# A first block of 512 tokens that starts with its first 256, and diagonals built by ScalarE in six pairs

## The chip, the cores and the metric

The kernel runs on one core of one Trainium2 chip. The metric is the device time of one execution in microseconds (us). Three runs of the kernel before gave 998.15, 998.85 and 999.84 us; the median is 998.85 us.

## The reference

Three parts run one after the other: a linear attention with a decaying state, and two small dense networks.

```
# r, k, v, w: batch 4, heads 8, 768 tokens, head width 48;  u: heads x 48
for t in range(S):
    cur   = outer(u * k[t], v[t])
    y[t]  = r[t] @ (state + cur)
    state = w[t][:, None] * state + outer(k[t], v[t])
x = y as 3072 tokens x 384
x = ((x @ w_a) * (x @ w_b)) @ w_out        # 384 -> 1536 -> 384
h = max(x @ w_in, 0);  x = (h * h) @ w_out2 # 384 -> 2048 -> 384
```

## The kernel before, in words

**Attention.** The 3072 tokens are 24 pairs of two chunks of 64 tokens. For a pair, VectorE (DVE in the rows) forms running products of the decay w (`at_scan`, L248) and their inverses (`at_recip`, L253, four instructions); GpSimd (POOL) multiplies them into k (`at_kr`, L257) and r (`at_rr`, L261). TensorE (PE) forms the scores (tile `sc`, L288 and L289), the transposed keys (`kt`, L299), the state's growth (`ds`, L311 and L313) and the outputs (`yp`, L332 and L333). The term with u needs one number per token and head: GpSimd multiplies r, k and u (L270), VectorE sums over the head (`dg`, L274), and GpSimd spreads the sums onto diagonals of the tile `ar` (`at_diag`, L278); VectorE then copies the scores above the diagonal into `ar` (`at_A2`, L294). `at_C2` (L320 to L324) carries the state to the next chunk.

**Weights.** The weights come as 64-bit floating-point words and are taken apart on the chip. The first network has 12 units (one per feature tile of 128), each with the words of w_a, w_b and w_out for that tile. A unit takes seven instructions of 128x1152: three by ScalarE (ACT; `z`, `raw`, then `w`, all L176) and four that change the bits (L191, L195, L200) or subtract (L209): L191 and L195 by VectorE, L200 and L209 by VectorE or GpSimd. L209 (`dec_lo`) is the last; TensorE can use the unit's tile `w` after it.

**Networks.** Every factor is split into a high and a low part, so one product takes three matmuls. Tokens go through in blocks: the first network's blocks are 384, 256, 384 and four times 512 tokens, the second's six times 512. For each block and feature tile, TensorE runs 9 matmuls for each of two products (tile `pa`, L358 to L360, in two PSUM buffers), ScalarE copies the first out (L365), VectorE multiplies it with the second (`mult`, L369), ScalarE and GpSimd split the result (`gh`, `gl`, L379), and 9 matmuls add it to three accumulators (`acc`, L385 to L387). The x of a block is written to DRAM by the attention, read back and split by ScalarE (`xh`) and VectorE (`xl`, L551).

**Order.** All instructions are put in order by a planner (`Plan.run`): it keeps a list of steps with engines, assumed durations, dependencies and a due time, and starts the ready step with the smallest due time whenever an engine is free. The due times come from a table of numbers (`KNOB`). What the planner starts on an engine stands in that engine's queue in this order, and each engine works its queue from front to back. A step with two engines in `ENG` goes to the one that is free first.

Of the kernel before, what the change touches and what calls it, by code (L numbers as in the profile page):

```python
# [21 lines left out]
C = 64  # L22
# [5 lines left out]
BLOCKS1 = [384, 256, 384] + [512] * 4  # L28
# [95 lines left out]
def fused_kernel(ctx, tc, tpk, natpk, vpk, v2pk, upk, cst, w1pk, w2pk, out):  # L124
# [226 lines left out]
    def prod(w, x, n):  # L351
# [4 lines left out]
        for k in range(KD):  # L356
            h, l = xh[:, k, 0:n], xl[:, k, 0:n]
# [14 lines left out]
    def split_hi(g, n, e="ACT"):  # L372
# [9 lines left out]
    def down(acc, d, w, g, n, first, last):  # L382
# [61 lines left out]
    def plan_pair(p):  # L444
# [33 lines left out]
        depA, acqA = [("kr", p), (("rr", 0), p), (("rr", 1), p)], [("at", (p, "A"))]  # L478
# [21 lines left out]
        add("B", {"PE": 0.41 * cold}, K["B"], lambda e: at_B(p), [("kr", p), "consts"], acq=[("at", (p, "B"))])  # L500
        add("B2", both(0, 448, *ENG["b2"]), K["B"], lambda e: at_B2(p, e), [("B", p)], acq=[("ky", (p, "k"))],
# [10 lines left out]
    def plan_dec(u, n, s, prio, deps):  # L512
# [7 lines left out]
        add(("ds", u, s), {"DVE": 0.75}, prio, lambda e: dec_sign(u, n), [("dz", u, s)], port=True)  # L520
# [4 lines left out]
        add(("dl", u, s), both(0, n, *ENG["dl"]), prio, lambda e: dec_lo(u, n, e), [("dh", u, s)], rel=[("z", (u, s))],  # L525
# [34 lines left out]
    def plan_step(s, j, f, nf, n, t, prev, w_up, w_down, units, dst):  # L560

        k = (s, j, f)
        need = [("dl", u, s) for u in units]
        before = (s, j, f - 1) if f else (s, j - 1, nf - 1) if j else (1, nb1 - 1, NF1 - 1) if s == 2 else ()
        add, mm, early = plan.add, 9 * t_mm(n), t - K["EARLY"]
        add(("ua", *k), {"PE": mm}, t, lambda e: put(("pa", *k), prod(part(w_up[0]), xs[s, j], n)),
            [("XS", s, j), ("ua", *before), ("ub", *before), *need], acq=[("ab", ("a", k))], rel=[] if s == 1 or f < nf - 1 else [("x", (s, j))])
        if s == 1:
# [3 lines left out]
            add(("ub", *k), {"PE": mm}, t, lambda e: put(("pb", *k), prod(part(w_up[1]), xs[s, j], n)),  # L572
                [("ua", *k)], acq=[("ab", ("b", k))], rel=[("x", (s, j))] if f == nf - 1 else [])
            add(("g", *k), both(0, n, "DVE"), early,
                lambda e: put(("g", *k), mult(box["a", *k], box["pb", *k], n)), [("a", *k), ("ub", *k), ("g", *before)],
                rel=[("ab", ("b", k))])
        else:
# [3 lines left out]
            add(("g", *k), both(0, n, "DVE"), early,  # L581
# [17 lines left out]
        if f < nf - 1:  # L599
            return  # L600
# [255 lines left out]
```

## Time and profile before

| what | us |
|---|---|
| median of three runs | 998.85 |
| profiled execution | 998.08 |
| its span | 996.2 |
| TensorE busy in the span | 940.4 (94%) |
| VectorE busy | 479.3 (48%) |
| ScalarE busy | 384.1 (39%) |
| GpSimd busy | 441.6 (44%) |

The profile covers one execution. Its span is the time from the first to the last recorded event on the core; the execution's own time is 1.9 us longer. A busy share is an average over the whole span, and the stages differ: TensorE has gaps in the first 130 us and none to speak of from there on, VectorE is the other way round. The granted clock in the windows is a share of TensorE's full speed.

### The profile page before, as it was taken

Reading aid. Unit: us, or ns where it says so; the run is one execution under the profiler, and the core shown is the slowest. Engines: PE = TensorE matmul, PEld = TensorE weight load, DVE = VectorE, ACT = ScalarE, POOL = GpSimd, SP = SyncE. Lnnn points to the kernel's source line nnn. Section 1 sums busy time; section 2 is a strip of 40 time slices with the busy share of each in tenths; the row PEclk is TensorE's granted clock in tenths of the full one; section 3 lists DMA queues with packets and bytes.
Section 4 is the critical chain, followed back from the end, with each engine's and each line's share of the span. In section 5 each row is a group of like instructions: output and inputs, shape, how many; then the busy total and the mean of one; then the engine's idle time right before and its main releaser. Section 6 shows DMA issues by size and latency. Waiting matters only on the chain.

```text
span 996.2 us, 14962 instructions
## 1 busy us (share of the span) xinstructions
PE 940.4 (94%) x5982; PEld 802.0 (81%) x5982; DVE 479.3 (48%) x585; ACT 384.1 (39%) x591; POOL 441.6 (44%) x359
## 2 busy tenths in 40 slices
PE   2668799999999999999999999999999999999997
PEld 2567699999988888888888888888888888888885
DVE  6889988875764444573212688721121211211111
ACT  1677443433422333332332677442233332323322
POOL 6733478886674545544122344333333333333332
PEclk9579899999999999999999999999999999999999
DMA  9995134652632332341111554010010000100001
GB/s 267 335 332 135 59 99 128 178 148 77 166 117 76 108 107 77 94 135 38 40 42 64 191 205 143 1 64 1 6 59 0 33 32 1 64 1 1 32 0 37
DMA packets 57791, 91.89 MB, mean 92 GB/s; under 512 B 23664, under 2 KB 31600, under 8 KB 57712
## 3 DMA queue, kind: packets, MB, share of 16 engines
q1 hardware_dynamic: 57712, 90.84, 29.6%
q8 instruction: 49, 0.80, 0.3%
q14 instruction: 30, 0.25, 0.1%
HBM read 76.66 MB, written 14.16 MB: 91 GB/s over the span
## 4 chain that ended last, share of the span: by engine, by line
PE 88%; DVE 5%; DMA 3%; ACT 1%; issue 1%; SPq 0%; POOL 0%; DVEq 0%; ACTq 0%
PE pa L358 16%; PE pa L360 16%; PE pa L359 16%; PE acc L385 11%; PE acc L387 11%; PE acc L386 11%; PE sc L288 2%; PE yp L332 2%; DVE w L209 1%; DVE z L200 1%; PE kt L299 1%; DMA ef<-in_tpk_dram 1%; PE ds L313 1%; DVE z L195 1%; DMA vs<-in_vpk_dram 1%
## 5 line engine op out<-in xcount | busy, mean ns | idle before, releaser
L379 POOL TENSOR_TENSOR gl<-a,gh 128x512 fp32r<-128x512 f32 (+2 forms) x180 | 235.2, 1308 | 474.4 <-ACT gh L176 469.9
L358 PE MATMUL pa<-xh,w 128*128 128x512 f32 (+2 forms) x792 | 296.3, 374 | 7.7 <-ACT w L176 3.3
L360 PE MATMUL pa<-xh,w 128*128 128x512 f32 (+2 forms) x792 | 295.1, 373 | 7.6 <-DVE w L209 7.6
L359 PE MATMUL pa<-xl,w 128*128 128x512 f32 (+2 forms) x792 | 294.4, 372 | 0.0
L365 ACT ACTIVATE a<-pa 128x512 f32<-128x512 f32 (+2 forms) x180 | 102.3, 569 | 277.8 <-PE pa L360 219.1
L385 PE MATMUL acc<-gh,w 128*128 128x512 f32 (+2 forms) x540 | 205.6, 381 | 0.0
L387 PE MATMUL acc<-gl,w 128*128 128x512 f32 (+2 forms) x540 | 202.7, 375 | 0.0
L386 PE MATMUL acc<-gh,w 128*128 128x512 f32 (+2 forms) x540 | 202.4, 375 | 0.0
L369 DVE TENSOR_TENSOR a<-a 128x512 f32<-128x512 f32 x96 | 67.9, 707 | 253.4 <-ACT a L365 253.4
L176 ACT ACTIVATE gh<-a 128x512 fp32r<-128x512 f32 (+2 forms) x180 | 108.3, 602 | 207.7 <-DVE a L369 161.9
L358 PEld LDWEIGHTS pa<-xh,w 128*128 128x128 f32 x792 | 150.1, 190 | 32.8 <-ACT w L176 4.3
L360 PEld LDWEIGHTS pa<-xh,w 128*128 128x128 f32 x792 | 150.2, 190 | 32.0 <-DVE w L209 9.2
L359 PEld LDWEIGHTS pa<-xl,w 128*128 128x128 f32 x792 | 150.1, 189 | 22.7 <-DVE xl L551 0.3
L369 DVE TENSOR_TENSOR a<-a,pa 128x512 f32<-128x512 f32 (+2 forms) x84 | 51.0, 607 | 140.8 <-PE pa L360 140.4
L385 PEld LDWEIGHTS acc<-gh,w 128*128 128x128 f32 x540 | 101.4, 188 | 17.9
L387 PEld LDWEIGHTS acc<-gl,w 128*128 128x128 f32 x540 | 101.5, 188 | 17.3 <-POOL gl L379 0.4
L386 PEld LDWEIGHTS acc<-gh,w 128*128 128x128 f32 x540 | 101.5, 188 | 16.2
L253 DVE RECIPROCAL ef<-ef 112x128 f32<-112x128 f32 x96 | 82.7, 913 | 0.5
L261 POOL TENSOR_TENSOR ar<-rk,ef 48x512 f32<-48x512 f32 (+1 forms) x48 | 59.0, 1230 | 27.8 <-DVE ef L248 10.0
L294 DVE COPY_PREDICATED ar<-mask,sc 64x512 f32<-64x512 int32 x48 | 35.2, 734 | 39.7 <-PE sc L289 37.7
L278 POOL TENSOR_TENSOR ar<-ident,dg 64x512 f32<-64x512 f32 x48 | 51.5, 1073 | 1.8
L209 DVE TENSOR_TENSOR w<-z,w 128x1152 fp32r<-128x1152 f32 (+1 forms) x22 | 37.2, 1691 | 6.0 <-ACT w L176 6.0
(54 smaller groups left out, 834.3 us busy)
## 6 DMA issues: line engine op xcount, KB each, us to landing
raw<-in_w1pk_dram SPq DMA_DIRECT2D x36, 384.0 KB, 6.8
raw<-in_w2pk_dram SPq DMA_DIRECT2D x32, 384.0 KB, 3.8
rk<-in_tpk_dram SPq DMA_DIRECT2D x24, 448.0 KB, 4.9
nat<-in_natpk_dram SPq DMA_DIRECT2D x24, 384.0 KB, 3.7
v<-in_v2pk_dram SPq DMA_DIRECT2D x24, 384.0 KB, 4.3
ef<-in_tpk_dram SPq DMA_DIRECT2D x24, 227.5 KB, 3.7
vs<-in_vpk_dram SPq DMA_DIRECT2D x48, 96.0 KB, 2.8
xd<-ys SPq DMA_DIRECT2D x48, 96.0 KB, 3.2
```

The lines of the kernel that those rows point to most:

```text
L176: nc.scalar.activation(out=out, in_=in_, func=ACTF.Copy, **({} if scale is None else {"scale": scale}))
L253: nc.vector.reciprocal(out=hv(inv(p), C)[:, h0:h0 + 2], in_=hv(ext(p), C + 1)[:, h0:h0 + 2, 1:])
L261: eng(e).tensor_tensor(out=hv(AR[p % 2][rows, c, :], C), in0=hv(RK[p][rows, TR:TK], C), in1=hv(ext(p), C + 1)[rows, :, 0:C], op=ALU.mult)
L358: nc.tensor.matmul(out=out, lhsT=blk(wh, k), rhs=h, start=(k == 0), stop=False)
L359: nc.tensor.matmul(out=out, lhsT=blk(wh, k), rhs=l, start=False, stop=False)
L360: nc.tensor.matmul(out=out, lhsT=blk(wl, k), rhs=h, start=False, stop=(k == KD - 1))
L365: nc.scalar.activation(out=a[:, 0:n], in_=P[:, 0:n], func=func, scale=scale)
L369: eng(e).tensor_tensor(out=a[:, 0:n], in0=a[:, 0:n], in1=b[:, 0:n], op=ALU.mult)
L379: eng(e).tensor_tensor(out=gl[:, 0:n], in0=g[:, 0:n], in1=gh[:, 0:n], op=ALU.subtract)
L385: nc.tensor.matmul(out=o, lhsT=blk(wh, d), rhs=gh[:, 0:n], start=first, stop=False)
L386: nc.tensor.matmul(out=o, lhsT=blk(wl, d), rhs=gh[:, 0:n], start=False, stop=False)
L387: nc.tensor.matmul(out=o, lhsT=blk(wh, d), rhs=gl[:, 0:n], start=False, stop=last)
```

## The change

The first network's blocks become six times 512 tokens. In the first block the first six feature tiles are done in two halves: the first 256 tokens (pairs 0 and 1) alone, the other 256 (pairs 2 and 3) later, each half with its own matmuls of 256 columns; the other six tiles are done with 512 columns. So that the accumulators start with 512 columns, the first matmul into each of the three is 512 wide, and ScalarE fills the missing half of its operand with zeros. For the first six pairs the diagonals are written by ScalarE, one 64x64 instruction for each head and chunk (16 a pair) in place of two by GpSimd, and the multiplication of k may go to VectorE. The first network's L200 and L209 (L207 and L216 in the new file) go to VectorE alone. Every due time has a new number.

```diff
-BLOCKS1 = [384, 256, 384] + [512] * 4
+BLOCKS1 = [512] * 6
+FIRST, APART = 256, 6
-KNOB = dict(START=13.52, FIRST=7.12, LEAD=18.8, DEC=4.0, DO=13.32, XO=5.1, X2=-14.73, D2=33.64, LW=15.56, LT=19.97,
+KNOB = dict(START=57.49, LEAD=22.53, DEC=8.23, U0=20.49, XO=44.77, X2=-72.12, D2=58.09, LW=19.06, LT=19.96, LV=0.24,
...
+           b2=("ACT",), gl=("POOL",), gh=("ACT",), dg=("POOL",), u1=("POOL",), ds=("DVE",))
+ENG0 = dict(ENG, kr=("DVE", "POOL"), dg=("ACT",), da=("DVE",), dl=("DVE",))
+NP0 = 6
...
     def at_diag(p, c, e="POOL"):
         rows = slice(c * C, c * C + C)
+        if e == "ACT":
+            for h in range(H):
+                nc.scalar.activation(out=AR[p % 2][rows, c, h * C:(h + 1) * C], in_=ident[rows, rows], func=ACTF.Copy,
+                                     scale=DG[p][rows, h:h + 1])
+            return
...
-            h, l = xh[:, k, 0:n], xl[:, k, 0:n]
+            h, l = xh[:, k, c0:c0 + n], xl[:, k, c0:c0 + n]
...
+        if fill:
+            copy("ACT", gh[:, n:NB], floor[:, 0:NB - n], 0.0)
...
-        o = acc[d][:, 0:n]
-        nc.tensor.matmul(out=o, lhsT=blk(wh, d), rhs=gh[:, 0:n], start=first, stop=False)
+        o, m = acc[d][:, c0:c0 + n], full if first else n
+        nc.tensor.matmul(out=acc[d][:, c0:c0 + m], lhsT=blk(wh, d), rhs=gh[:, 0:m], start=first, stop=False)
...
+        E0 = ENG0 if p < NP0 else ENG
...
-        add("kr", both(0, HC, *ENG["kr"]), K["kr"], lambda e: at_kr(p, e), [("LRK", p), *((("rec", k), p) for k in range(4))],
+        add("kr", both(0, HC, *E0["kr"]), K["kr"], lambda e: at_kr(p, e), [("LRK", p), *((("rec", k), p) for k in range(4))],
...
-        add(("da", u, s), {"DVE": t_dve(n) + 0.08, "POOL": t_pool(n)}, prio, lambda e: dec_add(u, n, e), [("dt", u, s)],
+        add(("da", u, s), both(0, n, *(ENG0 if s == 1 else ENG)["da"]), prio, lambda e: dec_add(u, n, e), [("dt", u, s)],
...
+            if j == 0 and f < APART:
+                h = FIRST
+                plan_step(1, j, f, NF1, 0, h, tau[0] + f * K["DA"], [(1, j, f - 1, 0)], *ws, ("XS", 1, j, h // 128 - 1))
+                plan_step(1, j, f, NF1, h, n - h, tau[0] + K["OB"] + f * K["DA"], [(1, j, f - 1, h)], *ws, ("XS", 1, j),
+                          start=False, after=[("dn", 1, j, 0, 0)] if f == 0 else [])
+                continue
```

The first place is VectorE's queue around the last subtraction of the twelve units (w11), the end of the decoding. Before (L209 is `dec_lo`, L248 and L253 are a pair's running products and inverses, L369 the multiplication of a feature tile, L320 the state):

```order
L209 TENSOR_TENSOR w10_1038<-z_955,w10_1038 128x1152
L200 ISA z_1017<-raw11_644,z_1017 128x2304
L369 TENSOR_TENSOR a_1035<-a_1035,pa_1046 128x384
L248 SCALAR_TENSOR_TENSOR ef_687<-ef_687,floor_85 112x520
L209 TENSOR_TENSOR w11_1080<-z_1017,w11_1080 128x1152
L253 RECIPROCAL ef_687<-ef_687 112x128 x4
L369 TENSOR_TENSOR a_1095<-a_1095,pa_1082 128x384
L369 TENSOR_TENSOR a_1125<-a_1125,pa_1137 128x384
L274 TENSOR_REDUCE dg_1181<-nat_695 128x8
L320 TENSOR_TENSOR ds_1190<-ds_1190,vs1_92 48x384
```

Now (line numbers are the new file's: L216 `dec_lo`, L255 and L260 products and inverses, L306 the masked copy, L381 the multiplication, L565 `xl`):

```order
L306 COPY_PREDICATED ar1_90<-mask_86,sc_1551 64x512 x2
L381 TENSOR_TENSOR a_1540<-a_1540,pa_1578 128x512
L216 TENSOR_TENSOR w10_1569<-z_1350,w10_1569 128x1152
L202 SCALAR_TENSOR_TENSOR z_1502<-z_1502,raw11_859 128x1152
L255 SCALAR_TENSOR_TENSOR ef_1298<-ef_1298,floor_85 112x520
L207 ISA z_1502<-raw11_859,z_1502 128x2304
L260 RECIPROCAL ef_1298<-ef_1298 112x128 x2
L381 TENSOR_TENSOR a_1646<-a_1646,pa_1650 128x512
L260 RECIPROCAL ef_1298<-ef_1298 112x128 x2
L216 TENSOR_TENSOR w11_1663<-z_1502,w11_1663 128x1152
L255 SCALAR_TENSOR_TENSOR ef_1473<-ef_1473,floor_85 112x520
L565 TENSOR_TENSOR xl_1674<-xl_1674,xh_1673 128x1536
```

Before, the queue holds the running products of six pairs and the inverses of five ahead of the last unit; now it holds both of nine pairs, and the x of the second block stands two places behind the last unit.

The second place is TensorE's queue at the attention of pair 4. Before, its transposes (`kt`, L299) stand behind the last product of unit 5, and the scores (`sc`) follow them:

```order
L358 MATMUL pa_800<-xh_429,w5_756 128x384
L359 MATMUL pa_800<-xl_430,w5_756 128x384
L360 MATMUL pa_800<-xh_429,w5_756 128x384
L299 MATMUL kt_813<-ident_84,rk_473 128x112 x4
L288 MATMUL sc_821<-ar0_89,rk_473 64x64
L289 MATMUL sc_821<-ar0_89,rk_473 64x64
```

The scores' 16 matmuls and an accumulation then stand ahead of the state's matmuls (`ds`). Now (L370 to L372 the products, L311 `kt`, L323 and L325 `ds`; kn is ScalarE's copy of kt):

```order
L370 MATMUL pa_839<-xh_338,w1_551 128x256
L371 MATMUL pa_839<-xl_339,w1_551 128x256
L372 MATMUL pa_839<-xh_338,w1_551 128x256
L311 MATMUL kt_853<-ident_84,rk_603 128x112 x4
L323 MATMUL ds_873<-v20_93,kn_868 48x96
L325 MATMUL ds_873<-v20_93,kn_868 48x96
```

The state's eight matmuls now follow the transposes directly, and the product behind them (pa_897, unit 4) takes the PSUM buffer of the product before last, pa_808. The multiplication that frees it stands on VectorE behind the four state instructions of this pair:

```order
L332 TENSOR_TENSOR ds_873<-ds_873,vs0_91 48x384
L333 TENSOR_TENSOR vs0_91<-ds_873,ef_569 48x384
L335 TENSOR_TENSOR ds_873<-ds_873,vs0_91 48x384
L336 TENSOR_TENSOR vs1_92<-ds_873,ef_569 48x384
L381 TENSOR_TENSOR a_836<-a_836,pa_808 128x256
L260 RECIPROCAL ef_655<-ef_655 112x128
L281 TENSOR_REDUCE dg_911<-nat_745 128x8
L260 RECIPROCAL ef_655<-ef_655 112x128
L381 TENSOR_TENSOR a_871<-a_871,pa_913 128x256
```

In VectorE's queue before, the multiplications of neighbouring feature tiles have parts of the decoding between them; here they have inverses and the state between them.

## Rows read from the trace of the kernel before

**Rows 1.** Windows: us; busy (instructions) of PE, PEld, DVE, ACT, POOL; PEclk; DMA share; GB/s
```profile
110.00:120.00 10.00, 5.41 (x45) 4.58 (x46) 8.12 (x7) 4.93 (x6) 5.71 (x3) 0.66 0.01 2
...
130.00:140.00 10.00, 10.00 (x84) 9.60 (x84) 7.06 (x9) 4.09 (x8) 8.80 (x8) 1.00 0.01 2
...
500.00:600.00 100.00, 100.00 (x443) 82.81 (x442) 47.74 (x42) 49.07 (x60) 31.78 (x19) 1.00 0.37 126
```

**Rows 2.** Waits, VectorE in 0 to 132 us, TensorE in 40 to 135
```profile
DVE ds L320 <- PE ds L313: 4.7, 1, 4.7
...
PE pa L360 <- DVE w L209: 7.6, 5, 3.6
```

**Rows 3.** Timeline of TensorE, start and duration: gap's end, spacings, second block's start
```profile
129.90 0.44 PE L358 MATMUL pa<-xh,w 128*128 128x384 f32 x1 [0.53 <-DVE a L369]
...
132.12 0.33 PE L385 MATMUL acc<-gh,w 128*128 128x384 f32 x1
...
133.85 0.33 PE L359 MATMUL pa<-xl,w 128*128 128x384 f32 x1
...
144.29 0.28 PE L358 MATMUL pa<-xh,w 128*128 128x256 f32 x1
...
148.02 0.28 PE L358 MATMUL pa<-xh,w 128*128 128x256 f32 x1
...
150.06 0.28 PE L360 MATMUL pa<-xh,w 128*128 128x256 f32 x1
```

**Rows 4.** Timeline of TensorE, its last matmul of the networks
```profile
988.88 0.39 PE L387 MATMUL acc<-gl,w 128*128 128x512 f32 x1
```

**Rows 5.** Timeline of VectorE: two sign instructions and the last decode
```profile
76.41 1.57 DVE L191 TENSOR_SCALAR raw<-raw 128x1152 int32<-128x1152 int32 x1
...
122.14 0.76 DVE L191 TENSOR_SCALAR raw<-raw 128x1152 int32<-128x1152 int32 x1
...
130.92 1.33 DVE L209 TENSOR_TENSOR w<-z,w 128x1152 fp32r<-128x1152 f32 x1
```

**Rows 6.** Lines of VectorE by form, 0 to 132.3 us: count, busy us, mean ns
```profile
L209 DVE TENSOR_TENSOR w<-z,w 128x1152 fp32r<-128x1152 f32 x11 | 18.5, 1686 | 2.1 <-ACT w L176 2.0
L253 DVE RECIPROCAL ef<-ef 112x128 f32<-112x128 f32 x21 | 17.9, 910 | 0.0
...
L200 DVE CUSTOM_DVE_ANT_0 z<-raw,z 128x2304 uint16<-128x2304 uint16 x10 | 15.1, 1514 | 0.0
L191 DVE TENSOR_SCALAR raw<-raw 128x1152 int32<-128x1152 int32 x12 | 13.3, 1115 | 0.3
L248 DVE TENSOR_TENSOR_SCAN ef<-ef,floor 112x520 f32<-112x520 f32 x6 | 7.9, 1323 | 4.5 <-DMA ef<-in_tpk_dram 4.5
L294 DVE COPY_PREDICATED ar<-mask,sc 64x512 f32<-64x512 int32 x10 | 7.2, 720 | 0.6 <-POOL ar L278 0.4
L369 DVE TENSOR_TENSOR a<-a,pa 128x384 f32<-128x384 f32 x10 | 5.5, 548 | 2.7 <-PE pa L360 2.6
...
L321 DVE TENSOR_TENSOR vs<-ds,ef 48x384 f32<-48x384 f32 x5 | 2.8, 559 | 0.2
...
L274 DVE TENSOR_REDUCE dg<-nat 128x8 f32<-128x384 f32 x5 | 2.7, 533 | 1.5 <-POOL nat L270 1.5
L551 DVE TENSOR_TENSOR xl<-xl,xh 128x384 fp32r<-128x384 f32 x3 | 1.7, 552 | 0.7 <-ACT xh L176 0.7
```

**Rows 7.** Window from the start to the last decode
```profile
0.00:132.30 132.30, 83.50 (x692) 74.84 (x693) 113.43 (x124) 69.69 (x87) 65.27 (x54) 0.83 0.69 215
```

**Rows 8.** Lines by form, whole span: multiplication on VectorE, copy-out on ScalarE
```profile
L365 ACT ACTIVATE a<-pa 128x512 f32<-128x512 f32 x144 | 86.0, 597 | 237.8 <-PE pa L360 181.8 <-POOL gl L379 56.1
...
L369 DVE TENSOR_TENSOR a<-a,pa 128x512 f32<-128x512 f32 x48 | 32.8, 684 | 123.2 <-PE pa L360 123.2
...
L369 DVE TENSOR_TENSOR a<-a,pa 128x256 f32<-128x256 f32 x12 | 5.0, 417 | 3.5 <-PE pa L360 3.4
L365 ACT ACTIVATE a<-pa 128x256 f32<-128x256 f32 x12 | 4.6, 384 | 16.8 <-PE pa L360 15.9 <-POOL gl L379 0.9
```

More of the change, by code (lines that the diff above doesn't have):

```diff
@@ L558, in plan_x, with plan_step @@
                      [("XH", *k), ("XH", *key) if last else (), ("XS", *key, i - 1)], port=True)
[L560 to L564, printed above, removed]
+    def plan_step(s, j, f, nf, c0, n, t, before, w_up, w_down, units, x_in="XS", start=True, after=()):
+        k = (s, j, f, c0)
+        need = [x for b in before for x in (("ua", *b), ("ub", *b))] + [("dl", u, s) for u in units]
         add, mm, early = plan.add, 9 * t_mm(n), t - K["EARLY"]
-        add(("ua", *k), {"PE": mm}, t, lambda e: put(("pa", *k), prod(part(w_up[0]), xs[s, j], n)),
-            [("XS", s, j), ("ua", *before), ("ub", *before), *need], acq=[("ab", ("a", k))], rel=[] if s == 1 or f < nf - 1 else [("x", (s, j))])
+        add(("ua", *k), {"PE": mm}, t, lambda e: put(("pa", *k), prod(part(w_up[0]), xs[s, j], c0, n)),
+            [x_in, *need], acq=[("ab", ("a", k))], rel=[] if s == 1 or f < nf - 1 else [("x", (s, j))])
         if s == 1:
@@ L589, in dn @@
-        def dn(e, ds):
-            for d in ds:
-                if f == 0:
-                    box.setdefault(("acc", s, j), {})[d] = new_acc(d)
-                down(box["acc", s, j], d, part(w_down), (box["gh", *k], box["gl", *k]), n, f == 0, f == nf - 1)
+            add(("g", *k), both(0, n, "DVE"), early, lambda e: put(("g", *k), mult(box["a", *k], box["a", *k], n)),
+                [("a", *k), *(("g", *b) for b in before)], port=True)
+        add(("gh", *k), both(0, n, *ENG["gh"]), early, lambda e: put(("gh", *k), split_hi(
+            box["g", *k], n, e, f == 0 and start and n < NB)),
+            [("g", *k), *(("gh", *b) for b in before)], acq=[("gg", k)])
@@ new lines, in plan_step, with dn @@
+        add(("gl", *k), both(0, n, *(ENG0 if (s, j) == (1, 0) else ENG)["gl"]), early,
+            lambda e: put(("gl", *k), split_lo(box["g", *k], box["gh", *k], n, e)),
+            [("gh", *k), *(("gl", *b) for b in before)], rel=[("a", k)], port=True)
+        def dn(d):
+            acc = box.setdefault(("acc", s, j), {})
+            if d not in acc:
+                acc[d] = new_acc(d)
+            down(acc, d, part(w_down), (box["gh", *k], box["gl", *k]), c0, n, f == 0 and start, f == nf - 1)
@@ L594, in plan_step, with plan_out @@
         t2 = t + K["T2"] * 9 * t_mm(n) * (2 if s == 1 else 1)
         for d in range(KD):
[L596 to L597 removed]
+            add(("dn", *k, d), {"PE": mm / 3}, t2, lambda e, d=d: dn(d),
+                [("gl", *k), ("dn", *k, d - 1), *(("dn", *b, d) for b in before), *((*x, d) for x in after)],
                 rel=[("gg", k)] if d == KD - 1 else [])
[L599 to L600 removed]
+    def plan_out(s, j, f, n, t, dst):
@@ L679, in finish @@
         for d in range(KD):
-            down(acc, d, w, (gh, gl), NG, first, last)
+            down(acc, d, w, (gh, gl), 0, NG, first, last, NG)
     def store(acc, dst):
```

96 lines of the change are left out of this document (47 added, 49 removed).

## The prediction

> **What bounds the kernel now.** I read the windows first, because a busy share over the whole span hides stages. TensorE is busy 5.41 of 10 us at 110 to 120 us, and all of every stretch from 130 us on; from 500 to 600 us it runs 443 matmuls of 512 columns without a gap [rows 1]. The last gap that it shows is 0.53 us, before 129.90 us [rows 3]. So from there on the kernel is the length of TensorE's queue, and the only way to lose or win time is before that point, or in the queue's length. In the stretch before, TensorE waits for VectorE's last decoding instruction (7.6 us in 5 waits [rows 2]), and VectorE is busy 113.4 of the first 132.3 us [rows 7]. The twelve units are decoded when L209 of the last one ends, at 130.92 + 1.33 = 132.3 us [rows 5]. VectorE's queue up to there sets the start; TensorE's queue sets the rest.
>
> I compare the kernels at one point: the first product of the second block, when the first block's products are all done. Before, this is at 144.29 us [rows 3]. TensorE ends its last matmul about 988.88 + 0.23 = 989.1 us [rows 4], so 844.8 us of queue lie behind the point. Behind the end lie 996.2 - 989.1 = 7.1 us of span and 1.9 us outside it, which I leave as they are.
>
> **TensorE's queue.** Spacing of matmuls: 512 columns, 100/443 = 0.2257 us [rows 1]; 384 columns, ten in 133.85 - 132.12 = 1.73, so 0.173; 256 columns, seventeen in 150.06 - 148.02 = 2.04, so 0.120 [rows 3]. A block takes 12 x 27 = 324 matmuls in the first network, and the second network 6 x 288 = 1728. Behind the point, before: 324 x 0.120 + 324 x 0.173 + (4 x 324 + 1728) x 0.2257 = 38.9 + 56.1 + 682.5 = 777.5 us. The other 67.3 us are attention: 18 whole pairs and the outputs of one, 18.3 pairs, 3.68 us each.
> Behind the same point in the changed queue: 9 accumulations of the last tile, 5 x 324 and 1728 matmuls of 512 columns, 3357 x 0.2257 = 757.7 us; and 16 pairs less the transposes of one, 15.9 x 3.68 = 58.5 us. Together 816.2 us, 28.6 less than before. 2.3 pairs of these (8.8 us) and the larger block are work that has moved ahead of the point; over the whole run the queue is shorter by only about 2 us, since 2106 matmuls do the first network in place of 2268 (block by block at these spacings: 38.9 + 36.6 for the first 512 tokens, 73.1 for each other). So the change is even if the second block starts at 144.3 + 28.6 = 172.9 us.
>
> **VectorE's queue.** I count what stands ahead of the last L209 in either order, and price the difference by the means that the same instructions had in the same stretch before, collisions included [rows 6]. It has three running products more (9 for 6) x 1.323 = 4.0; 16 inverses more (36 for 20; the twenty-first in the row is behind the last decode) x 0.910 = 14.6; 4 head sums x 0.533 = 2.1; 6 masked copies x 0.720 = 4.3; 10 state instructions x 0.56 = 5.6; one `xl` x 0.55. Of the multiplications 12 of 256 columns x 0.417 and 5 of 512 x 0.684 [rows 8] stand where 10 of 384 x 0.548 stood: 2.9. GpSimd no longer takes two L200 (2 x 1.514 = 3.0) and one L209 (1.7). The k multiplication now stands on VectorE in two pairs; 112x512 has no row there, so it is bounded by `xl` of 384 columns, 0.55, and the multiplication of 512, 0.68: 0.65 each, 1.3. Sum 40.1 us. All rows of that stretch add up to 119.1 us where the busy time is 113.4 [rows 7], since neighbours overlap, so I take 0.952 of it: 38.2 us.
> If VectorE waits as long as before, the last unit is decoded at 132.3 + 38.2 = 170.4 us. Then the last tile's two products (18 x 0.2257 = 4.1), a pair's transposes and three accumulations (about 1) run before the second block's first product: 175.5 us. The x of that block stands two places behind the last decode (1.3 us, and `xl` of 1536 columns, about 2 us), and is ready in that time. 175.5 is 2.6 us later than 172.9.
>
> **What I cost at nothing or bound.** The wait is the open number: 132.3 - 113.4 = 18.9 us before. Less: the first pair now comes alone, ahead of the second, and the 4.7 us for its state matmuls [rows 2] should shrink. More: the new order chains VectorE and TensorE at pair 4. There the product pa_897 cannot start before VectorE has worked four state instructions (4 x 0.56) and a multiplication, which themselves wait for state matmuls queued behind transposes and a ScalarE copy, with TensorE idle meanwhile; then the next two multiplications wait for these products. I take these to cancel. For the ends: waits of 8 us, with the queue dense since three more pairs fill it, give -11 us; waits that grow with the queue (18.9 x 170/132 = 24.3), +5.4.
> The 96 diagonals of 64 columns on ScalarE have no row. From 256 columns (0.384) and 512 (0.597) [rows 8] the slope is 0.83 ns a column and 64 columns cost 0.22: 3.5 us a pair, where ScalarE was busy 69.7 of 132.3 us [rows 7]. Nearly all of it is covered; below nothing it can't be, as GpSimd's time for them ran beside VectorE's too. Its end is 4 us, if all of two pairs' diagonals stand in the chain (7 us) and replace GpSimd's two slots (2 us each at most). I take 0. The three wider matmuls (3 x 0.106) and the zero fill (0.38) are in the stretch that VectorE bounds: 0.
> Here a rule speaks against the change. The Trainium skill's page "ScalarE: Activation LUTs" (section What ACT_TABLE_LOAD costs) gives an ACTIVATE 186 ns with immediate operands and about 93 ns more for each per-partition pointer, which these carry as their scale; by it one would be an estimated 0.33 us and a pair 5.3 us. That would make my sum 1 to 2 us later, where pairs 0 and 4 wait; no row here shows such an operand.
> The sum: 998.1 + 2.6 = 1000.7, so 1001 us.
>
> **Rivals.**
> *Faster, 991 us.* VectorE's waits fall to 8 us: the decode ends at 159.5, the second block starts at 164.6, 8.3 us ahead of even. And collisions may fall too. A sign instruction takes 0.76 us alone and 1.57 when GpSimd works on SBUF beside it [rows 5]; its mean, 1.115, and L209's, 1.686 against 1.33 alone, show 12 x 0.36 + 11 x 0.35 = 8 us of such delays in rows whose means I have carried on. For: twelve diagonals and three decoding steps leave GpSimd. Against: GpSimd does the inputs of three more pairs in the same stretch, and VectorE's share of decoding rises.
> The Trainium skill's "SBUF — State Buffer" (section Who interferes with whom) calls it an exclusive lock between GpSimd and a VectorE instruction with two SBUF inputs or in a two-port mode, and lets ScalarE wait on no one; by that rule the moved diagonals collide with nothing. The 1.57 us row agrees.
> *Even, 998 us.* The two movements cancel exactly: waits 2.6 us shorter, and nothing is left. The early start then does not do what it says: TensorE begins earlier and stands still later.
> *Slower still, 1009 us.* TensorE's gap at pair 4 lasts until the clock falls, as at 110 to 120 us (5.41 us busy, granted 0.66 [rows 1], between 1.2 and 2.4 GHz). At 1.2 GHz a product of nine 256-column matmuls takes 2.2 us in place of 1.1; VectorE's next multiplications wait for three of them (3.3 us), and the same at two later spots where scores and outputs wait for masked copies. It decides from about 3 us of VectorE waiting on TensorE; +8 us.
>
> **How the numbers follow.** My forecast, 1001 (own range 997 to 1006): 0.42. Faster, 991 (985 to 996.8): 0.33. Even, 998: 0.10. Slower still, 1009 (1006 to 1014): 0.15. About 0.2%, 2 us, is what a measurement tells from no change: 996.9 to 1000.9. The profiled execution lies 0.8 us under the median, within that. The forecast's lower part falls into "same". Faster 0.33, same 0.22, slower 0.45. The range: 988 to 1010.
>
> **What would show it.** Right: the last decode's L209 (now L216) ends between 166 and 175 us, the second block's first product comes at 171 to 180, and 816 us of gapless TensorE follow it to the last matmul. The first product comes earlier than before, and TensorE has gaps of several us between 80 and 100 us. Wrong: a last decode before 165 us, with mean L209 and sign instructions well under 1.69 and 1.12 us, or VectorE idle under 10 us up to there (then the faster case); gaps in TensorE behind the second block's start would break the step on the rest of the queue.

## The result and the profile after

The changed kernel takes 1005.26 us (median of six runs, 1002.93 to 1006.15); the kernel before takes 999.58 beside it (six runs, 998.15 to 1000.25). The ratio is 1.0055, 95% interval 1.0042 to 1.0068: slower by about 5.5 us. The profiled execution took 1003.95 us, with a span of 1002.2.

First the windows, with the columns of [rows 1]. The first answers to [rows 7].

```profile
0.00:169.90 169.90, 119.72 (x1116) 102.82 (x1116) 157.75 (x177) 106.71 (x213) 94.49 (x71) 0.92 0.69 207
80.00:90.00 10.00, 5.41 (x45) 4.74 (x43) 9.77 (x9) 7.62 (x12) 5.43 (x3) 0.89 0.86 298
90.00:100.00 10.00, 6.70 (x39) 6.39 (x38) 8.90 (x14) 6.41 (x21) 4.88 (x5) 0.60 0.27 94
...
300.00:400.00 100.00, 99.61 (x707) 82.15 (x706) 54.03 (x74) 30.78 (x51) 57.10 (x47) 1.00 0.37 107
...
100.00:180.00 80.00, 71.00 (x619) 59.27 (x618) 75.47 (x76) 35.89 (x54) 57.51 (x36) 1.00 0.35 95
```

VectorE is busy 157.75 of the 169.9 us up to the last decode, where it was busy 113.43 of 132.3. TensorE has little left to idle: 9.0 us between 100 and 180, almost nothing afterwards.

TensorE's timeline (start, duration, and in brackets the idle time before and what ended it), answering to [rows 3, 4]; then VectorE's last decode [rows 5], and the GpSimd subtraction that ran beside it.

```profile
168.19 0.39 PE L401 MATMUL acc<-gh,w 128*128 128x512 f32 x1
...
171.04 0.50 PE L402 MATMUL acc<-gl,w 128*128 128x512 f32 x1 [2.46 <-POOL gl L393]
...
172.08 0.39 PE L370 MATMUL pa<-xh,w 128*128 128x512 f32 x1
...
174.93 0.60 PE L311 MATMUL kt<-ident,rk 112*128 112x112 f32 x4 [0.62 <-POOL rk L264]
...
178.11 0.39 PE L370 MATMUL pa<-xh,w 128*128 128x512 f32 x1
...
994.57 0.39 PE L402 MATMUL acc<-gl,w 128*128 128x512 f32 x1
```

```profile
168.58 1.29 DVE L216 TENSOR_TENSOR w<-z,w 128x1152 fp32r<-128x1152 f32 x1
...
167.80 3.19 POOL L393 TENSOR_TENSOR gl<-a,gh 128x512 fp32r<-128x512 f32 x1 [1.97 <-ACT gh L180]
```

The last decode ends at 168.58 + 1.29 = 169.87 us and the second block starts at 178.11. From there to the end of the last matmul it is 994.57 + 0.23 - 178.11 = 816.7 us. Behind it lie 1002.2 - 994.8 = 7.4 us of span and 1.75 outside. The start is where the time went: it comes 178.11 - 144.29 = 33.8 us later, and the queue behind it is 844.8 - 816.7 = 28.1 us shorter (28.6 were predicted). The 5.7 us between these two are nearly the whole loss; the profiled executions differ by 1003.95 - 998.08 = 5.87.

VectorE's lines up to the last decode, answering to [rows 6] (L255, L260, L216, L207 and L198 here are L248, L253, L209, L200 and L191 there):

```profile
L260 DVE RECIPROCAL ef<-ef 112x128 f32<-112x128 f32 x36 | 31.5, 918 | 0.1
L216 DVE TENSOR_TENSOR w<-z,w 128x1152 fp32r<-128x1152 f32 x12 | 19.2, 1599 | 0.4 <-ACT w L180 0.2
L202 DVE SCALAR_TENSOR_TENSOR z<-z,raw 128x1152 int32<-128x1152 int32 x12 | 19.1, 1596 | 0.1
L207 DVE CUSTOM_DVE_ANT_0 z<-raw,z 128x2304 uint16<-128x2304 uint16 x12 | 18.7, 1556 | 0.1
L255 DVE TENSOR_TENSOR_SCAN ef<-ef,floor 112x520 f32<-112x520 f32 x10 | 17.2, 1722 | 2.2 <-DMA ef<-in_tpk_dram 2.2
L198 DVE TENSOR_SCALAR raw<-raw 128x1152 int32<-128x1152 int32 x12 | 14.0, 1166 | 1.2 <-ACT z L180 1.2
```

The same shift (L202) before, which was no row of the prediction:

```profile
L195 DVE SCALAR_TENSOR_TENSOR z<-z,raw 128x1152 int32<-128x1152 int32 x12 | 16.9, 1412 | 0.0
```

The reader is to see two things. The idle column is nearly empty, so VectorE hardly waits any more. And two kinds of instruction that read two SBUF operands have grown, running products and shifts (1.41 to 1.60 us), while the inverses, with one operand, stayed at 0.91 to 0.92. The running products' 1.72 has in it a tenth one of 2.29 that begins 0.1 us before the window's end; the nine before it took 1.66 in the mean, where it was 1.32 before. The subtraction (L216) also reads two operands and did not grow: 1.69 before, 1.60 now.

### The profile page after: what moved, and what is told of

The parts are those of the page before. It is cut to its first block, busy times and chain, and to the rows that moved or that the text cites. A ratio compares the mean times of both kernels' runs of the same rounds, so it can differ in the third digit from the quotient of the medians.

```text
span 1002.2 us, 14663 instructions
## 1 busy us (share of the span) xinstructions
PE 942.8 (94%) x5820; PEld 783.0 (78%) x5820; DVE 488.2 (49%) x585; ACT 406.0 (41%) x674; POOL 436.9 (44%) x334
## 4 chain that ended last, share of the span: by engine, by line
PE 81%; DMA 7%; DVE 6%; ACT 2%; issue 1%; POOL 1%; SPq 1%; DVEq 0%; POOLq 0%; ACTq 0%
PE pa L370 15%; PE pa L371 15%; PE pa L372 15%; PE acc L400 11%; PE acc L402 10%; PE acc L401 10%; DMA xd<-ys 2%; DMA xl<-xd 2%; PE yp L344 1%; PE sc L300 1%; DMA raw<-in_w1pk_dram 1%; DVE ef L260 1%; DVE z L202 1%; DVE ar L306 1%; DVE z L207 1%
## 5 line engine op out<-in xcount | busy, mean ns | idle before, releaser
L393 POOL TENSOR_TENSOR gl<-a,gh 128x512 fp32r<-128x512 f32 (+1 forms) x174 | 241.4, 1388 | 476.0 <-ACT gh L180 463.3
L370 PE MATMUL pa<-xh,w 128*128 128x512 f32 (+1 forms) x756 | 291.5, 386 | 10.7 <-DVE a L381 5.1
L371 PE MATMUL pa<-xl,w 128*128 128x512 f32 (+1 forms) x756 | 288.8, 382 | 1.5 <-DVE xl L565 1.5
L372 PE MATMUL pa<-xh,w 128*128 128x512 f32 (+1 forms) x756 | 288.6, 382 | 1.1 <-DVE w L216 1.1
L180 ACT ACTIVATE gh<-a 128x512 fp32r<-128x512 f32 (+1 forms) x174 | 107.2, 617 | 253.8 <-DVE a L381 205.5
L377 ACT ACTIVATE a<-pa 128x512 f32<-128x512 f32 (+1 forms) x174 | 101.2, 582 | 252.2 <-PE pa L372 188.4
L400 PE MATMUL acc<-gh,w 128*128 128x512 f32 (+1 forms) x522 | 203.1, 389 | 0.0
L402 PE MATMUL acc<-gl,w 128*128 128x512 f32 (+1 forms) x522 | 199.7, 383 | 2.8 <-POOL gl L393 2.8
L401 PE MATMUL acc<-gh,w 128*128 128x512 f32 (+1 forms) x522 | 199.5, 382 | 0.0
L381 DVE TENSOR_TENSOR a<-a 128x512 f32<-128x512 f32 x96 | 68.8, 718 | 257.3 <-ACT a L377 257.3
L370 PEld LDWEIGHTS pa<-xh,w 128*128 128x128 f32 x756 | 144.1, 191 | 40.2 <-DVE a L381 5.8
L372 PEld LDWEIGHTS pa<-xh,w 128*128 128x128 f32 x756 | 144.2, 191 | 28.5 <-DVE w L216 1.3
L381 DVE TENSOR_TENSOR a<-a,pa 128x512 f32<-128x512 f32 (+1 forms) x78 | 50.0, 642 | 115.5 <-PE pa L372 113.9
L260 DVE RECIPROCAL ef<-ef 112x128 f32<-112x128 f32 x96 | 83.6, 918 | 0.4
L306 DVE COPY_PREDICATED ar<-mask,sc 64x512 f32<-64x512 int32 x48 | 35.3, 735 | 71.0 <-PE sc L301 70.5
L277 POOL TENSOR_TENSOR nat<-nat 128x384 f32<-128x384 f32 x24 | 30.3, 1263 | 34.0 <-DMA nat<-in_natpk_dram 32.6
```

Source lines behind the costliest of these rows:

```text
L180: nc.scalar.activation(out=out, in_=in_, func=ACTF.Copy, **({} if scale is None else {"scale": scale}))
L260: nc.vector.reciprocal(out=hv(inv(p), C)[:, h0:h0 + 2], in_=hv(ext(p), C + 1)[:, h0:h0 + 2, 1:])
L370: nc.tensor.matmul(out=out, lhsT=blk(wh, k), rhs=h, start=(k == 0), stop=False)
L371: nc.tensor.matmul(out=out, lhsT=blk(wh, k), rhs=l, start=False, stop=False)
L372: nc.tensor.matmul(out=out, lhsT=blk(wl, k), rhs=h, start=False, stop=(k == KD - 1))
L377: nc.scalar.activation(out=a[:, 0:n], in_=P[:, 0:n], func=func, scale=scale)
```

## The experiments

The theory: VectorE's queue up to the last decode, lengthened by the attention of three more pairs and by collisions with GpSimd, sets the start of the second block. The rivals: ScalarE's diagonals; TensorE's gap and slow clock at pair 4; a chain through several engines in which VectorE's work alone decides little. Each run is compared with runs of the kernel before on the same chip. The intervals are some 1.0 to 1.7 us to either side, so a difference of 1 us between two runs is not told apart, and one of 2 us barely. Beside the change the kernel before took 999.58 us; beside e1 to e4 it took 999.39, beside e5 to e8 999.04, beside e9 to e11 998.85 and beside e12 999.58. So the last two columns give the distance from the change twice: between the medians, and as the difference of the two ratios times 999.58, which is the fairer one.

| run | median, us | ratio to before, 95% interval | against the change's 1005.26 | by the ratios |
|---|---|---|---|---|
| e1 inverses out | 1000.06 | 1.0007 (0.9997 to 1.0017) | -5.2 | -4.8 |
| e2 inverses twice | 1019.06 | 1.0193 (1.0180 to 1.0207) | +13.8 | +13.8 |
| e3 diagonals by GpSimd | 1008.66 | 1.0092 (1.0078 to 1.0106) | +3.4 | +3.7 |
| e4 less GpSimd | 1002.98 | 1.0033 (1.0022 to 1.0045) | -2.3 | -2.2 |
| e5 pair 4's chain | 1004.22 | 1.0053 (1.0036 to 1.0070) | -1.0 | -0.2 |
| e6 chain, inverses out | 998.39 | 0.9991 (0.9980 to 1.0001) | -6.9 | -6.4 |
| e7 later pairs, signs | 999.58 | 1.0004 (0.9993 to 1.0015) | -5.7 | -5.1 |
| e8 all three | 998.63 | 0.9997 (0.9986 to 1.0007) | -6.6 | -5.8 |
| e9 pair 4's chain, clean | 1004.05 | 1.0048 (1.0035 to 1.0061) | -1.2 | -0.7 |
| e10 later pairs, chain | 1001.82 | 1.0032 (1.0020 to 1.0044) | -3.4 | -2.3 |
| e11 before, ScalarE diagonals | 1004.79 | 1.0055 (1.0041 to 1.0068) | | |
| e12 before, some of them | 1001.67 | 1.0025 (1.0013 to 1.0038) | | |

**e1 and e2: VectorE's work taken away, and added.**

```diff
 def at_recip(p, q):                       # e1
+    if 4 <= p <= 8:
+        if q == 0:
+            nc.vector.memset(inv(p), 1.0)
+        return
 ...
-    nc.vector.reciprocal(...)             # e2
+    for _ in range(2 if 4 <= p <= 8 else 1):
+        nc.vector.reciprocal(...)
```

> The changed kernel with the inverses of pairs 4 to 8 (20 instructions of 0.918 us on VectorE) left out: one fill with 1 (0.49 us by the fill of 128x520) stands in each pair's place, so k is not scaled in those pairs. VectorE's queue up to the last decode gets 20 x 0.918 - 5 x 0.49 = 15.9 us shorter; no other queue changes. Theory (VectorE's queue sets the start of the second block): the last decode comes 12 to 16 us earlier; the time falls by less, 8 to 13 us, since TensorE idles only 9 us between 100 and 180 us and about 19 us between 40 and 100, and can use only what it idles: about 993 us. Rival (the chain through ScalarE, TensorE and GpSimd sets it, and VectorE's 12 us of waits only grow): under 4 us faster, 1001 or more.

> The changed kernel with each inverse of pairs 4 to 8 formed twice (the second writes the same numbers): VectorE's queue up to the last decode gets 20 x 0.918 = 18.4 us longer, nothing else. Theory: nearly one for one, 15 to 18.4 us slower, about 1021 us, and the second block starts that much later. Rival (VectorE has room: 12.1 us of waits before the last decode, and the chain runs through other engines): 6 us slower or less, about 1011.

Added work comes through at 13.8 of 18.4 us, 1.2 under the theory's range and far above the rival's 6. The last decode, here in e2, ends at 187.79 + 1.29 = 189.08, 19.2 us later. GpSimd's low part `gl` is done before that here, and TensorE does not wait for it behind the decode; the second block starts at 194.25, 5.2 us after the decode's end where it was 8.2 in the change. That is 16.1 us later than in the change, and the profiled spans differ by 1017.7 - 1002.2 = 15.5:

```profile
185.03 1.28 POOL L394 TENSOR_TENSOR gl<-a,gh 128x512 fp32r<-128x512 f32 x1 [3.94 <-ACT gh L180]
...
187.79 1.29 DVE L216 TENSOR_TENSOR w<-z,w 128x1152 fp32r<-128x1152 f32 x1
...
194.25 0.39 PE L371 MATMUL pa<-xh,w 128*128 128x512 f32 x1
```

Removed work comes through at 5.2 of 15.9 us (4.8 by the ratios), and both theories missed it: mine by 2.8 us, the rival by 1.2. The windows of e1 and VectorE's largest wait up to its last decode:

```profile
0.00:166.10 166.10, 122.01 (x1113) 105.81 (x1114) 145.10 (x162) 105.38 (x212) 91.22 (x71) 0.95 0.70 212
...
100.00:180.00 80.00, 76.02 (x684) 63.75 (x684) 68.70 (x71) 37.51 (x57) 58.27 (x39) 1.00 0.39 105
```

```profile
DVE a L385 <- PE pa L376: 7.5, 6, 2.2
```

VectorE's idle time rises from 12.1 to 166.1 - 145.1 = 21.0 us; 7.5 of it is for products of TensorE, 1.0 in the change (the 10.6 in e6's expectation has 3.1 in it that lie behind the last decode). Pair 4 shows it most plainly. Its four inverses stood between 72.4 and 76 us; without them the same subtraction comes at the same time. The change, then e1:

```profile
67.83 1.23 DVE L255 TENSOR_TENSOR_SCAN ef<-ef,floor 112x520 f32<-112x520 f32 x1
...
72.37 2.57 DVE L260 RECIPROCAL ef<-ef 112x128 f32<-112x128 f32 x3
...
82.02 1.35 DVE L216 TENSOR_TENSOR w<-z,w 128x1152 fp32r<-128x1152 f32 x1
```

```profile
74.12 0.42 DVE L385 TENSOR_TENSOR a<-a,pa 128x256 f32<-128x256 f32 x1 [0.96 <-PE pa L376]
75.06 0.55 DVE L285 TENSOR_REDUCE dg<-nat 128x8 f32<-128x384 f32 x1 [0.52 <-POOL nat L281]
...
81.92 1.35 DVE L216 TENSOR_TENSOR w<-z,w 128x1152 fp32r<-128x1152 f32 x1
```

At the end of the decoding TensorE is what holds e1. The last decode ends at 166.05 us there, 3.8 earlier, but TensorE is still at its accumulations then; it reaches the last tile's products at 168.30, and the second block starts at 174.35, again 3.8 us earlier. TensorE's idle time from 100 to 180 us falls from 9.0 to 4.0; its wait for `gl`, 2.46 us in the change, is 0.26.

So VectorE is the bound, with little room to the next one: a longer queue is paid at three quarters, a shorter one gives back a third.

**e3 and e4: GpSimd's work added, and taken away.**

```diff
+SWAP = {(("dg", c), p): "POOL" for c in range(2) for p in range(6)}     # e3
...
-            ops[i][3](e)
+            ops[i][3](SWAP.get(ops[i][0], e))
...
 def at_u1(p, i, e="POOL"):                                              # e4
+    if i == 1 and p < 9:
+        return
```

> The changed kernel with the diagonals of the first six pairs built by GpSimd again (12 instructions, 1.66 us by the mean of the other pairs'), everything else in the same order. ScalarE loses 24.1 us, GpSimd gains 20 us. Theory (ScalarE's diagonals are hidden, and VectorE's queue decides): no gain from ScalarE; VectorE collides more: by 18 us of excess of its rows over their shortest, with 100 us of GpSimd's work beside it, 0.18 us for each us of GpSimd, so 1 to 4 us slower, about 1007. Rival (the 0.33 us of each ScalarE diagonal, in the chain of pairs 0 and 4, made the change slower): 1 to 4 us faster.

> The changed kernel with GpSimd's second multiplication for the u term (nat by u_sb, 1.25 us each) left out in the first nine pairs, so u counts as 1 there: 11.3 us of GpSimd's work less in the stretch up to the last decode, VectorE's instructions the same. Theory (VectorE's queue, lengthened by collisions with GpSimd): at 0.18 us of VectorE's time for each us of GpSimd's, 2 us faster (1 to 3), about 1003, and the means of the shift, subtraction and scan rows fall. Rival 1 (collisions cost nothing that counts): within 0.5 us. Rival 2 (GpSimd's own chain sets the start): 5 us faster or more.

Both came out as the theory had them, though e4's interval and the change's still overlap. VectorE's lines of e3, where its instructions are the same:

```profile
L203 DVE SCALAR_TENSOR_TENSOR z<-z,raw 128x1152 int32<-128x1152 int32 x12 | 20.6, 1717 | 0.1
L208 DVE CUSTOM_DVE_ANT_0 z<-raw,z 128x2304 uint16<-128x2304 uint16 x12 | 19.8, 1650 | 0.1
...
L199 DVE TENSOR_SCALAR raw<-raw 128x1152 int32<-128x1152 int32 x12 | 16.1, 1344 | 0.7 <-ACT z L181 0.6
```

The shift rises by 0.12 us, the custom step by 0.09, the sign by 0.18, each twelve times: 4.7 us, and the last decode ends 5.5 us later:

```profile
174.05 1.29 DVE L217 TENSOR_TENSOR w<-z,w 128x1152 fp32r<-128x1152 f32 x1
```

So in this order ScalarE's diagonals help by 3.4 us on balance; that rival falls. e4's profile was its slowest run of nine (1006.05 us, with 4.6 us of waiting for the decay's inputs where the change waits 2.2), and its last decode ends later than in the change, at 172.59; so only its median and its means are used: sign 1.094 us, custom step 1.500, shift 1.571, all shorter than in the change.

```profile
L202 DVE SCALAR_TENSOR_TENSOR z<-z,raw 128x1152 int32<-128x1152 int32 x12 | 18.8, 1571 | 0.1
...
L207 DVE CUSTOM_DVE_ANT_0 z<-raw,z 128x2304 uint16<-128x2304 uint16 x12 | 18.0, 1500 | 0.1
...
L198 DVE TENSOR_SCALAR raw<-raw 128x1152 int32<-128x1152 int32 x12 | 13.1, 1094 | 1.6 <-ACT z L180 1.5
```

**e5, e9 and e6: TensorE's gap at pair 4.** Steps are moved in the finished order, each behind the one named second (`g` multiplication, `a` copy-out, `C` state matmuls, `C2` the state on VectorE, `LV2` the load of v):

```diff
+MOVES = [(('g', 1, 0, 0, 256), ('dl', 4, 1)),
+         (('a', 1, 0, 1, 256), ('dr', 9, 1)),
+         (('C', 4), ('ub', 1, 0, 1, 256)),
+         (('C2', 4), ('g', 1, 0, 1, 256)),
+         (('LV2', 6), ('C', 4))]          # the last in e9 alone
```

> The changed kernel with four steps at pair 4 in another place: the multiplication that frees the product's buffer (second half of tile 0) moves up VectorE's queue ahead of two decodings and the state, the copy-out for tile 1's second half moves up ScalarE's, and the state's matmuls and VectorE's four state instructions move behind the next two products. No work is added or left out. It takes away what TensorE waits for at 87 us (3.3) and 93.5 us (3.3) and the half clock behind them. Theory (VectorE's queue sets the end; it waited only 1 us for TensorE there): 0 to 2 us faster, about 1004. Rival (TensorE's gap at pair 4 and its slow clock made the change slower): 4 to 7 us faster, about 1000.

> Both edits: pair 4's steps in the other places, and the inverses of pairs 4 to 8 left out as before (one fill with 1 each). With the inverses out alone, VectorE waited 10.6 us for TensorE's products in place of 1.0 and the time fell by 5.2 us for 15.9 us of work. Theory now (two engines in one chain: VectorE is the bound until it is shortened, then TensorE's late products of 80 to 100 us are): together more than the sum of each alone, 3 to 6 us faster than the inverses out alone, 994 to 997. Rival (TensorE's queue from 100 us on is full whatever happens at pair 4): within 1 us of 1000.

> Pair 4's steps in the other places again, with one difference to the earlier run of this kind: there the load of pair 6's v stood ahead of pair 4's state matmuls, which then read it and waited 4.4 us for it; here that load is issued behind them, where it belongs, and nothing is changed in what is computed. Theory (VectorE's queue sets the end, TensorE's gap at pair 4 is worth at most what VectorE waited there, 1 us): 0 to 2 us faster than the change, 1003.5 to 1005. Rival (the gap and its half clock cost the change its time): 4 us or more faster, 1001 or less.

In e5 and e6, and in e8 below, pair 6's v was loaded over pair 4's before its use, so pair 4's state is made from pair 6's v. e5 and e9 lie within 1.2 us of the change, as the theory had it, and e6 is 1.7 us faster than e1, under the 3 to 6 expected and over the rival's 1; each is near what can be told apart. But the gap did not go, so the rival is not fully tested. The change, then e9:

```profile
87.09 0.28 PE L323 MATMUL ds<-v,kn 128*48 128x96 f32 x1 [3.29 <-ACT kn L180]
...
93.47 0.58 PE L370 MATMUL pa<-xh,w 128*128 128x256 f32 x1 [3.30 <-DVE a L381]
```

```profile
87.45 0.28 PE L331 MATMUL ds<-v,kn 128*48 128x96 f32 x1 [0.96 <-ACT kn L188]
...
90.52 1.26 ACT L188 ACTIVATE z<-raw 128x1152 f32<-128x1152 f32 x1 [3.12 <-DVE w L224]
...
93.11 0.36 ACT L385 ACTIVATE a<-pa 128x256 f32<-128x256 f32 x1
...
93.52 0.58 PE L378 MATMUL pa<-xh,w 128*128 128x256 f32 x1 [5.20 <-ACT a L385]
```

The two waits of 3.3 us became one of 5.2: the copy-out that frees the buffer stands on ScalarE behind a decoding step, which waits for VectorE to free a tile `z`. What the gap itself costs stays open.

**e7, e8 and e10: less ahead of the last decode, without leaving work out.** The scans of pairs 8 to 10 wait for the second block's `xl`, the u multiplications of pairs 9 and 10 for the tenth tile's low part. In e7 and e8 ScalarE also does five signs, by a multiplication by 0.0 where VectorE masked the bit, so these units' weights are not the reference's. e8 also has e5's moves, e10 those of e9 and the signs on VectorE; of the three only e10 computes what the reference does.

```diff
-        add("scan", ..., [("LT", p)], port=True)
+        add("scan", ..., [("LT", p), *([("XS", 1, 1)] if p in (8, 9, 10) else [])], port=True)
...
+SWAP = {("ds", u, 1): "ACT" for u in range(7, 12)}     # e7, e8
```

> The changed kernel, nothing left out, with less of VectorE's work ahead of the last decode: the running products and inverses of pairs 8 to 10 are kept behind the second block's x (two scans of 1.72 us and four inverses of 0.92 stood ahead), the sign instructions of units 7 to 11 (1.17 us each) are done by ScalarE right behind the unit's first step, and GpSimd's u multiplications of pairs 9 and 10 stand behind the tenth unit's low part. VectorE: 3.4 + 3.7 + 5.8 = 12.9 us less; ScalarE 6 us more. Theory: like the inverses left out, about a third to a half comes through, 4 to 6 us faster, about 1000. Rival (ScalarE's added work stands in the chain of products; or the second block's x, which waits for pair 7's outputs, is late whatever is decoded): under 2 us faster.

> The two real relocations together: pair 4's steps in the other places, the later pairs' inputs behind the second block's x, five sign instructions on ScalarE. Nothing is left out. Theory (VectorE and TensorE bound each other in turn, so both must be relieved): 6 to 10 us faster than the change, 995 to 999, at or a little under the kernel before. Rival (pair 7's outputs and the x of the second block, read back at 163.5 us and split by 173.7 us, come no earlier): 1001 or more.

> Pair 4's steps in the other places (with pair 6's load behind) and the running products and inverses of pairs 8 to 10 behind the second block's x; the signs stay on VectorE, nothing is left out. VectorE has 7.1 us less ahead of the last decode, ScalarE the same as in the change. Theory (VectorE's queue, of which a third to a half comes through): 3 to 5 us faster than the change, 1000 to 1002, level with before or just behind. Rival (only the five signs on ScalarE made the difference in the runs with them): under 1.5 us faster.

By the medians all three fell into the theory's ranges. By the ratios e7 alone does (5.1 us); e8 stands just under its 6 to 10, and e10, with 2.3, between its theory's 3 and its rival's 1.5. e7 and e8 stand level with the kernel before, but with other weights in five units; e10 is 0.2 to 0.4% slower than it. e8's last decode, the second block's `xl`, VectorE's largest wait after 100 us, and its window:

```profile
163.75 1.35 DVE L230 TENSOR_TENSOR w<-z,w 128x1152 fp32r<-128x1152 f32 x1
169.25 2.52 DVE L579 TENSOR_TENSOR xl<-xl,xh 128x1536 fp32r<-128x1536 f32 x1 [4.15 <-ACT xh L194]
```

```profile
DVE xl L579 <- ACT xh L194: 4.2, 1, 4.2
```

```profile
100.00:180.00 80.00, 76.30 (x644) 64.15 (x642) 67.05 (x69) 41.01 (x59) 54.71 (x39) 0.99 0.37 103
```

The decode ends 4.8 us earlier than in the change. Now VectorE waits for the second block's x, and TensorE idles only 3.7 us between 100 and 180. Beyond these 3.7 us more can only come from the time before 100 us, which none of these three runs changed (TensorE is busy 40.8 to 41.0 of the 60 us from 40 to 100 in the change and in all three).

**e11 and e12: the diagonals alone, in the order of before.**

```diff
+SWAP = {(("dg", c), p): "ACT" for c in range(2) for p in range(6)}       # e11
+SWAP = {(("dg", c), p): "ACT" for c in range(2) for p in (0, 2, 4, 5)}   # e12
```

> The kernel before with one part of the change alone: the diagonals of the first six pairs by ScalarE, everything else and every order as before. GpSimd loses 10 to 12 instructions of 1.2 us in the first 132 us, ScalarE gains up to 24.1 us where it was busy 70. Putting them back on GpSimd in the changed kernel cost 3.4 us. Theory (GpSimd's collisions lengthen VectorE's queue, ScalarE has room): 1 to 3 us faster than before, 996 to 998. Rival (ScalarE's 4 us a pair stand in the chain of pairs 0 to 2, which in this order come early one behind the other): 0 to 3 us slower than before.

> The kernel before with the diagonals by ScalarE in pairs 0, 2, 4 and 5 alone; in pairs 1 and 3 GpSimd writes them as before. With all of the first six pairs on ScalarE, VectorE's masked copies waited 3.5 us for the diagonals of pair 1 and 3.5 us for those of pair 3 (a decoding step of ScalarE stood between the two halves), and for no others. Theory (ScalarE's diagonals cost only where they are awaited, and relieve GpSimd elsewhere): the 7.5 us of waits are gone; up to 8 diagonals of 1.2 us less on GpSimd at 0.2 us of VectorE's time each us: 0 to 2 us faster than before, 997 to 999.5. Rival (ScalarE's 16 instructions a pair delay its decoding steps wherever they stand): 2 us slower or more, 1001 and up.

My theory failed in both. The rival held in e12; in e11 it had the direction right, but its range of 0 to 3 us ends at half of the 5.9 measured. VectorE's window up to the last decode and its largest wait in e11, and the timeline:

```profile
0.00:138.80 138.80, 84.74 (x691) 76.21 (x692) 109.99 (x124) 88.71 (x167) 52.74 (x44) 0.84 0.67 205
```

```profile
DVE ar L300 <- ACT ar L281: 7.5, 3, 3.5
```

```profile
34.08 0.73 DVE L300 COPY_PREDICATED ar<-mask,sc 64x512 f32<-64x512 int32 x1 [3.47 <-ACT ar L281]
...
137.47 1.32 DVE L210 TENSOR_TENSOR w<-z,w 128x1152 fp32r<-128x1152 f32 x1
```

VectorE's busy time falls by 113.4 - 110.0 = 3.4 us, as the collisions said; its waits rise from 18.9 to 28.8, most of it for diagonals. In e12 these waits are gone, but ScalarE's decoding steps come later:

```profile
DVE w L210 <- ACT w L177: 3.4, 3, 1.8
...
DVE raw L192 <- ACT z L177: 2.4, 3, 1.7
```

```profile
133.23 1.33 DVE L210 TENSOR_TENSOR w<-z,w 128x1152 fp32r<-128x1152 f32 x1
```

For the signs VectorE waited 0.3 us before [rows 6]. The last decode ends 2.3 us later than before, and the time is 2.1 us longer. The same instructions that help by 3.4 us in one order cost 5.9 in the other: there VectorE had few waits on ScalarE, and the diagonals made some.

## Why the prediction was right

The forecast was 1001 us, slower, and the reason held: VectorE's queue moved the second block by more than TensorE's queue lost behind it. But that reason makes only 2.6 of the 5.7 us by which the start is too late (169.87 + 5.1 = 175.0 against 144.3 + 28.1 = 172.4); the other 3.1 came from a step that the prediction had too short.

| step | predicted | measured |
|---|---|---|
| queue behind the second block's start | 816.2 | 816.7 |
| VectorE busy up to the last decode | 113.4 + 38.2 = 151.6 | 157.75 |
| VectorE's waits up to it | 18.9 | 12.1 |
| last decode ends | 170.4 | 169.87 |
| second block starts | 175.5 | 178.11 |
| k multiplication, 112x512 on VectorE | 0.65 | 0.69 |
| behind the last matmul, in and outside the span | 9.0 | 9.15 |

**TensorE's queue** was right to 0.5 us, and nothing interrupts it: 99.61 of 100 us from 300 on.

**VectorE's queue** came out within 0.5 us by two errors that cancel, which is luck. I carried on the old means. Their growth is 9 x 0.34 (running products) + 12 x 0.18 (shifts) + 12 x 0.04 (custom steps) + 12 x 0.05 (signs) + 36 x 0.008 (inverses) - 12 x 0.09 (subtractions) = 5.5 us, most of the difference of the busy times, 157.75 - 151.6 = 6.1. The Trainium skill's "SBUF — State Buffer" (section Who interferes with whom) says that a VectorE instruction with two SBUF inputs contends with a GpSimd instruction that reads SBUF, and one with a single input, outside the two-port modes, does not. The trace agrees for the running products, with 1.66 us in the mean and 1.23 where GpSimd was idle as it began (67.83 us, shown with e1), and for the inverses, with 0.918. The subtraction that the prediction calls alone (130.92 us, 1.33) had a GpSimd multiplication beside it from 131.13 us on; the size stands, for the one at 90.25 us, with GpSimd idle, took 1.34. e3 and e4 put the price at some 0.2 us for each us of GpSimd's work (3.4 for 12 diagonals of 1.54, 2.3 for 11.3). The waits fell by 6.8, not to the 8 us of the faster rival: the 4.7 us for the first state matmuls are gone [rows 2], as the text had it, but the pair-4 chain did not give them back.

**The step that failed** is the one from the last decode to the second block: 5.1 us predicted, 8.2 measured. It took the tile's products to start as soon as the unit is decoded. But the products stand in TensorE's queue behind an accumulation that waits for GpSimd's `gl`. That ran from 167.80 for 3.19 us, with VectorE's last subtraction and a running product beside it, and TensorE stood still for 2.46 us. The products began at 172.08 in place of 169.9, and the transposes waited 0.62 us more for GpSimd: 2.8 of the 3.1 us. e2 shows the step without these two waits: 5.2 us, as predicted. No run took them away and left VectorE's queue as it is; in e8 and e10, which order these steps otherwise, the wait for `gl` is 1.1 us.

**What I cost at nothing.** The diagonals: right for this order (e3), and not a property of the instruction, as e11 shows. Their duration was not right. The row:

```profile
L287 ACT ACTIVATE ar<-ident,dg 64x64 f32<-64x64 f32 x96 | 24.1, 332 | 9.9 <-DVE dg L281 9.7
```

By the rows I had 0.22 us each and 3.5 a pair. One takes 0.332, which is the estimate from the Trainium skill's "ScalarE: Activation LUTs" (section What ACT_TABLE_LOAD costs; 0.33). But neighbours overlap, and 24.1 / 96 = 0.25 us each makes 4.0 a pair, nearer the rows' sum than the 5.3 of the estimate. The estimate left out what the same section of the Trainium skill states, that ACTIVATEs one behind the other overlap by about 93 ns; the trace agrees (0.332 - 0.25 = 0.08 us).

**The rivals.** *Faster* fell with the waits (12.1 us, not 8) and with the collisions, which grew in all (the 5.5 us above). *Slower still* was right that the gap comes and the clock falls: TensorE is busy 5.41 and 6.70 of 10 us from 80 to 100, granted 0.89 and 0.60. Before, the first product came at 61.46 us, now at 49.67, and part of what it gains is idled there.

```profile
61.46 0.69 PE L358 MATMUL pa<-xh,w 128*128 128x384 f32 x1 [2.96 <-ACT xh L176]
```

```profile
49.67 0.58 PE L370 MATMUL pa<-xh,w 128*128 128x256 f32 x1 [1.12 <-ACT xh L180]
```

But its price was wrong: VectorE waits for those products 1.0 us in all, not 8, since it has other work in its queue. With inverses taken out of that work (e1) it waits 7.5 us for TensorE's products, 3.0 of them behind this gap and the rest at 74, 115, 137 and 164 us. So the two bounds lie close to each other; no experiment beat the kernel before by more than its interval.

## What to carry to other kernels

Work that is moved ahead of the point where the bottleneck starts is free only if the engine that feeds that point has the time; count its queue up to the point, with its neighbours' collisions, before counting what the bottleneck saves behind it. When a trace shows one engine with hardly a wait, ask what it would wait for next: here a third of what was taken off it came through. And an instruction moved to a less busy engine is judged by who waits for it in that order, not by the engine's busy share.

## What the runs showed that I had not expected

- The same 16 ScalarE diagonals a pair gain 3.4 us in one order and lose 5.9 in another.
- Taking four inverses (3.5 us, for a fill of 0.5) out of VectorE's queue at 72 us changed nothing ten microseconds later: 82.02 against 81.92.
- A GpSimd subtraction of 512 columns took 3.19 us beside VectorE's subtraction and a running product, and 1.29 us beside VectorE's inverses at 179.13 us:

```profile
179.13 1.29 POOL L393 TENSOR_TENSOR gl<-a,gh 128x512 fp32r<-128x512 f32 x1 [2.16 <-ACT gh L180]
```
